# Loads of queries and keys in 1 KB runs, transposed by head, low parts on VectorE, and other weights of a list scheduler: attention and two expert layers on one core

## The chip, the core and the metric

The kernel runs on one core of a Trainium2 chip. The metric is the time of one execution on the device in microseconds (us), and the time before is the median of three runs. Five engines work side by side, each in the order in which its instructions were written: TensorE (PE in the profile, with its weight loads as PEld), VectorE (DVE), ScalarE (ACT), GpSimd (POOL) and SyncE (SP), whose queue issues nearly all DMAs.

## The reference

Three layers follow each other. Attention has 4 batches of 8 heads, 576 positions and 64 values per head, with a causal window of 64 positions. The second layer works on 2304 tokens; the third sends each token whose skip score is positive to one of eight experts.

```python
scores = np.matmul(q, k.transpose(0, 1, 3, 2)) / np.sqrt(D)
scores = np.where((rel >= 0) & (rel < 64), scores, -1e9)
attn = softmax(scores)
x = np.matmul(attn, v)                      # as [2304, 512]
h = x @ w_in                                # [512, 2048], float64 weights
x = (h * np.tanh(np.log1p(np.exp(h)))) @ w_out
e = np.argmax(x @ w_gate, axis=1)           # 8 experts
y = gate * (np.maximum(x @ w1[e], 0) @ w2[e])
out = np.where(x @ w_skip > 0, x + y, x)
```

## The kernel before, in words

The tokens form six blocks of 384 (`NB`), and each block has four pairs of heads. A pair's path is: load queries and keys (`load_nat` for the first eight pairs, `load_dvt` later), transpose them on TensorE into PSUM (`nat_T`, twice, keys and queries), copy them out (`nat_k`, `nat_q`), scores (`att_S`), mask and maximum on VectorE (`att_max`), exponentials on ScalarE (`att_exp`), normalizing (`att_norm`), a transpose (`att_PT`), and the product with the values (`att_PV`). Products that need more than TensorE's short float format take a high and a low part of each operand: `x_part` and `wide_H`/`wide_L` make them, and `expert_H`/`expert_L`, `xs_H`/`xs_L` do so for the third layer. A low part is the operand minus its high part, one subtraction of 128x512 (line 341 or 1082).

The second layer goes over 16 chunks of 128 hidden columns for each block, 96 chunks `c` in all. `L1(c)` is 12 products of 128x384 into a PSUM tile `ph` of two buffers; `m_min`, `m_exp`, `m_square`, `m_ln`, `m_r` and `m_g` form the gate on VectorE and ScalarE, and `m_g` frees `ph`; `L2(c)` adds the result into three PSUM tiles `po`, one for each 128 tokens, over the 16 chunks of the block. In block 0, `L2` takes `g` whole; later it takes high and low parts. At the end of a block `x_evac` copies `po` out to one of only three tiles `xs`, the router finds each token's expert, and `scatter` writes `xs` to a table of slots in memory. So the three `xs` tiles, and with them `po`, wait for the scatters of the block before. A scatter waits until every slot was filled once (`fill_slots`, 17 DMAs in rounds of two, each round behind a write by `fill_zero` and the landing of the round before).

The weights of the second layer come as 64-bit numbers (`wide_load`) and are converted on VectorE and ScalarE (`wide_e`, `wide_a`, `wide_l`, `wide_s`), 32 tiles in the first blocks. After the last block comes the bend to the third layer: router, scatter, and a product with 0/1 matrices (`select`) that gathers the first expert's tokens. Then the experts follow one another.

The order is not written by hand. `Plan` lists tasks with engines and costs, dependencies, buffers and due times; `order` simulates the lists greedily and picks, for the engine that is free first, the ready task with the earliest due time. Due times come from `T0`, `D0`, `D1`, `US`, `UO`, `WO`, `LO` and are shifted by kind of task through `LATE`; the engine of a task is chosen by cost with `PRICE0`, `PRICE`, `PRICE2` (by time) and `LEAN`. `keep_warm` puts small products (`warm`) where the plan has TensorE idle before the first `L2` and in the bend.

The diff touches the tables above, `load_nat`, `nat_T` and task costs:

```python
for r in range(4):
    PE.transpose(o[:, r, :nr], t[:nr, r].rearrange("p j d -> p (j d)"), ident[:nr, :nr])
```

Of the kernel before, what the change touches and what calls it, by code (L numbers as in the profile page):

```python
# [9 lines left out]
F32 = mybir.dt.float32  # L10
# [15 lines left out]
T0, D0, D1, US, UO, WO, LO = 20.57, 3.54, 4.21, 1.68, 5.52, 2.09, 3.4  # L26
# [6 lines left out]
FILL_AT, FILL_BY = 21, 6.0  # L33
# [125 lines left out]
TW0 = 30.94  # L159
PRICE0 = dict(P=0.0, V=2.28, A=0.5, G=-0.5, S=0.0)  # L160
TW = 309.39
PRICE2 = dict(P=0.0, V=1.26, A=2.91, G=0.0, S=0.0)
PRICE = dict(P=0.0, V=2.33, A=1.47, G=0.63, S=0.0)
LAT = {("V", "V"): 0.13, ("A", "A"): 0.13, ("A", "V"): 0.14, ("V", "A"): 0.13, ("P", "P"): 0.05}
LATE = dict(wl=-9.64, wa=-0.1, wo=-3.47, ws=-4.07, wH=-11.22, lqk=-4.23, nT=-11.43, S=-14.23, ex=-0.53, nm=-4.0, PT=0.94, Pe=7.68, xH=-13.18, L1=2.57, L2=0.89, me=1.15, n=-4.49, mn=-0.61, ln=-5.67, r=-7.61, g=3.04, gH=3.02, xe=2.94, rT=1.62, re=-6.31, rl=2.98, rs=-1.25, lg=13.87, ro=-1.68, eH=16.04, rc=1.8, PV=-0.21, wL=2.42, ga=-3.86, sL=-1.97, xo=13.29, eL=4.54, m2=6.01, bl=18.08, wb=-0.93, ke=-20.26, m1=16.67, se2=-11.46, sl=7.64, el=-0.26, qT=2.69, fz=-9.43, bt=-20.62, se=-13.56, sH=11.09, sd=-1.3, wg=-1.88, tg=9.05, fs=-2.81, xgH=-0.09, sm=9.36, oh=-8.74, su=7.71, xL=-4.21, we=3.45, pl=-8.44, gL=2.75, pi=-2.04, co=-1.2, pm=-0.37, dm=8.62, kT=-2.92, fi=-2.37, mx=3.12, L2t=14.66, ep=-14.67, rq=0.13, lv=-0.43)
LEAN = {('kT', 'A'): 0.38, ('qT', 'A'): -1.31, ('nm', 'A'): 0.39, ('xH', 'A'): -1.88, ('wo', 'A'): -0.82, ('wH', 'A'): -0.15, ('n', 'A'): -1.04, ('re', 'A'): -1.33, ('xe', 'A'): 0.36, ('nm', 'G'): 0.37, ('wL', 'G'): -2.59, ('gL', 'G'): 1.14}
SLACK = dict(P=0.04, V=0.0, A=0.0, G=0.17, S=0.0)
# [3 lines left out]
def tile_kernel(  # L171
# [15 lines left out]
    B, H, S, D = q.shape  # L187
# [31 lines left out]
    for p0 in (0, 64):  # L219
        sl = maskA[p0:p0 + 64]  # L220
# [146 lines left out]
    def one(eng, cost):  # L367
        return [(eng[0], eng[1], cost)]
# [44 lines left out]
    def load_nat(pr):  # L413
        blk, hp = divmod(pr, 4)
        nq = rqp.tile([128, 4, 2, D], F32, tag="rk", name="nq", bufs=4)
        nk = rqp.tile([128, 4, 2, D], F32, tag="rk", name="nk", bufs=4)
        r0 = 0
        for g, n, b, s0 in runs(blk):
            t0 = max(s0 - 64, 0)
            nr = (s0 + 192 * n - t0) // 4  # L420
            hs = slice(2 * hp, 2 * hp + 2)
            SP.dma_start(out=nk[r0:r0 + nr], in_=k[b, hs, t0:s0 + 192 * n].rearrange("j (p r) d -> p r j d", r=4))
            SP.dma_start(out=nq[48 * g:48 * (g + n)], in_=q[b, hs, s0:s0 + 192 * n].rearrange("j (p r) d -> p r j d", r=4))
            r0 += nr
        nat[pr] = (nq, nk, r0)

    def nat_T(pr, i):
        t = nat[pr][i]
        nr = nat[pr][2] if i else 96
        if pr < 4:  # L430
            o = ps_o.tile([128, 4, 128], F32, tag=f"po{i}", name="tqk")
        else:
            o = ps_s.tile([128, 4, 128], F32, tag="ps", name="tqk")
        for r in range(4):
            PE.transpose(o[:, r, :nr], t[:nr, r].rearrange("p j d -> p (j d)"), ident[:nr, :nr])
        tqk[pr, i] = o
# [142 lines left out]
    for pr in range(NU // 2):  # L579
        t = unit_time(2 * pr) - 5  # L580
        if pr < NPE:
            T(("lqk", pr), one(SS, 1.8 if len(runs(pr // 4)) == 1 else 2.3), lambda e, pr=pr: load_nat(pr), lat=2.3,
              get=[("rk", ("nq", pr)), ("rk", ("nk", pr))], due=t, t0=.7)
            for i in (1, 0):
                T(("nT", pr, i), one(PP, .36), lambda e, pr=pr, i=i: nat_T(pr, i), after=[("lqk", pr)] + ([("S", pr - 1)] if pr else []),
                  get=[(f"po{i}" if pr < 4 else "ps", ("tqk", pr, i))], use=[("nq", pr) if i == 0 else ("nk", pr)])
        else:
            T(("lqk", pr), one(SS, 3.6 if len(runs(pr // 4)) == 1 else 7.2), lambda e, pr=pr: load_dvt(pr), lat=2.3,
              get=[("rq", ("nq", pr)), ("rk", ("nk", pr))], due=t - 5)
        nd = sum(3 if r[3] == 0 else 2 for r in runs(pr // 4))  # L590
        T(("lv", pr), [("S", SP, max(1.6, .5 * nd))], lambda e, pr=pr: load_v(pr, e), lat=2.3,
          get=[("vt", ("vt", pr))], due=unit_time(2 * pr))
# [104 lines left out]
    for f in range(NF):  # L697
        for kind in ("in", "out"):
# [3 lines left out]
            T(("wl", key), [("S", SP, 1.46)], lambda e, key=key, i=i: wide_load(key, i, e), lat=2.3, due=t - 8)  # L702
# [428 lines left out]
    for n in range(32):  # L1131
# [10 lines left out]
        T(("eL", key), [("G", G, 1.23), ("V", V, .6)], lambda e, key=key: expert_L(e, key), after=[("eH", key)],  # L1142
# [287 lines left out]
```

## Time and profile before

| | |
|---|---|
| median of three runs | 695.97 us (695.02 to 697.1) |
| profiled execution | 695.74 us, of which the span is 693.6 us |
| TensorE busy | 678.2 us, 98% of the span |
| VectorE busy | 450.6 us, 65% |
| ScalarE busy | 392.2 us, 57% |
| GpSimd busy | 74.2 us, 11% |
| mean granted clock of TensorE | 0.991 |

Busy time is what the profiler counts for instructions on each engine; products overlap, so starts tell more than durations. An idle stretch before an instruction is put down to what released it last.

### The profile page before, as it was taken

How to read it: one execution, taken by the hardware profiler on the slowest of the kernel's cores; microseconds unless marked ns; L12 is line 12 of the kernel's file. 1: busy time of each engine (PE TensorE's matmuls, PEld its weight loads, DVE VectorE, ACT ScalarE, POOL GpSimd, SP SyncE). 2: the span in 40 equal slices, each digit the busy share in tenths (PEclk: the TensorE clock that was granted, in tenths of full speed). 3: DMA queues.
4: the chain of work that ended last, by engine and by line, in shares of the span. 5: the costliest groups of instructions: out<-in, count | busy, mean ns of one | idle time of the engine just before them, and what ended most of it. 6: DMA issues, size and time to landing. Idle time of an engine off the chain costs nothing. (4 is left out here: it accounts for less than half of the span.)

```text
span 693.6 us, 13440 instructions
## 1 busy us (share of the span) xinstructions
PE 678.2 (98%) x4884; PEld 582.5 (84%) x4884; DVE 450.6 (65%) x1268; ACT 392.2 (57%) x963; POOL 74.2 (11%) x133
## 2 busy tenths in 40 slices
PE   6899999999999999999999999999999999999996
PEld 6787776788888888888888888888898898998994
DVE  4999999876766556556776656457668563674352
ACT  5899787677667676686555555445552242232130
POOL 3000000000020001000020002013244011020011
PEclk9999999999999999999999999999998999999999
DMA  9999986877432312232311000054473677677200
GB/s 189 270 280 303 267 156 138 202 150 158 79 74 44 83 36 53 46 92 49 78 31 41 30 1 26 1 182 138 129 231 115 228 245 259 238 290 271 89 25 21
DMA packets 150492, 92.53 MB, mean 133 GB/s; under 512 B 111869, under 2 KB 128253, under 8 KB 150416
## 3 DMA queue, kind: packets, MB, share of 16 engines
q1 hardware_dynamic: 147696, 87.11, 47.7%
q0 software_dynamic: 2720, 4.42, 1.8%
q8 instruction: 45, 0.74, 0.5%
q14 instruction: 31, 0.25, 0.1%
HBM read 73.96 MB, written 17.86 MB: 132 GB/s over the span
## 5 line engine op out<-in xcount | busy, mean ns | idle before, releaser
L735 PE MATMUL ph<-xH,w 128*128 128x384 f32 x768 | 220.6, 348 | 0.2
L786 PE MATMUL po<-w,gH 128*128 128x512 f32 x480 | 154.4, 403 | 0.0
L735 PEld LDWEIGHTS ph<-xH,w 128*128 128x128 f32 x768 | 140.9, 188 | 7.0 <-issue 1.9
L735 PE MATMUL ph<-xL,w 128*128 128x384 f32 x384 | 130.0, 338 | 0.0
L743 ACT ACTIVATE u<-u 128x384 f32<-128x384 f32 x96 | 50.3, 524 | 122.2 <-DVE u L740 122.2
L786 PEld LDWEIGHTS po<-w,gH 128*128 128x128 f32 x480 | 87.2, 188 | 17.2 <-issue 1.6
L786 PE MATMUL po<-w,gL 128*128 128x512 f32 x240 | 95.1, 396 | 0.0
L762 DVE SCALAR_TENSOR_TENSOR u<-u,ph 128x384 f32<-128x384 f32 x80 | 44.1, 551 | 71.6 <-ACT u L756 71.2
L735 PEld LDWEIGHTS ph<-xL,w 128*128 128x128 f32 x384 | 72.2, 188 | 4.1 <-issue 2.2
L740 DVE TENSOR_SCALAR u<-ph 128x384 f32<-128x384 f32 x96 | 53.1, 553 | 18.1 <-PE ph L735 17.2
L1218 PEld LDWEIGHTS ph<-xgT,w 128*128 128x128 f32 x512 | 63.8, 190 | 1.0 <-DVE xgT L317 0.4
L1218 PE MATMUL ph<-xgT,w 128*128 128x144 f32 x512 | 64.3, 286 | 0.3 <-DVE xgT L317 0.3
L771 DVE TENSOR_TENSOR gL<-u,gH 128x384 fp32r<-128x384 f32 x80 | 46.5, 581 | 17.2 <-ACT gH L315 14.2
L529 ACT ACTIVATE P<-P,mx 128x128 f32<-128x128 f32 x144 | 55.6, 389 | 0.9 <-DVE mx L522 0.9
L786 PEld LDWEIGHTS po<-w,gL 128*128 128x128 f32 x240 | 45.1, 188 | 11.3 <-DVE gL L771 0.6
L1245 ACT ACTIVATE hH<-ph 128x288 fp32r<-128x288 f32 x32 | 13.2, 411 | 68.9 <-PE ph L1218 56.5
L747 ACT ACTIVATE u<-u 128x384 f32<-128x384 f32 x96 | 50.4, 525 | 2.9
L753 ACT ACTIVATE u<-u 128x384 f32<-128x384 f32 x96 | 50.2, 523 | 2.3
L756 ACT ACTIVATE u<-u 128x384 f32<-128x384 f32 x96 | 50.2, 522 | 2.3
L786 PE MATMUL po<-w,g 128*128 128x512 f32 x96 | 44.0, 594 | 0.0
L1262 PE MATMUL po<-w,hH 128*128 128x512 f32 x128 | 42.6, 414 | 0.0
L341 DVE TENSOR_TENSOR w<-st,w 128x512 fp32r<-128x512 f32 x48 | 34.3, 732 | 0.7
(156 smaller groups left out, 985.6 us busy)
## 6 DMA issues: line engine op xcount, KB each, us to landing
st<-in_moe_w_dram SPq DMA_DIRECT2D x64, 256.0 KB, 6.2
w<-in_moe_w_dram SPq DMA_DIRECT2D x32, 512.0 KB, 5.5
w<-in_moe_w_in_dram SPq DMA_DIRECT2D x16, 512.0 KB, 7.1
w<-in_moe_w_out_dram SPq DMA_DIRECT2D x16, 512.0 KB, 6.6
out_dram<-xs SPq DMA_DIRECT2D x18, 256.0 KB, 2.4
xg<-xg_d SPq DMA_DIRECT2D x16, 257.0 KB, 4.0
ca<-w SPq DMA_DIRECT2D x16, 256.0 KB, 3.7
xg_d<-nothing SPq DMA_DIRECT2D x16, 256.0 KB, 5.0
```

The source lines that it names most:

```text
L529: A.activation(P[:, i], P[:, i], AF.Exp, bias=mx[:, 0, u % 2, i:i + 1], scale=-1.0, accum_out=mx[:, 1, u % 2, i:i + 1])
L735: PE.matmul(phs[c], a[:, kk], b[:, kk], start=kk == 0 and n == 0, stop=kk == NK - 1 and n == len(terms) - 1)
L740: V.tensor_scalar(u, phs[c], 20.0, None, op0=ALU.min)
L743: A.activation(us[c], us[c], AF.Exp)
L747: A.activation(us[c], us[c], AF.Square, bias=1.0)
L753: A.activation(us[c], us[c], AF.Ln, scale=0.5, bias=half_t[c])
L756: A.activation(us[c], us[c], AF.Exp, scale=-1.0)
L762: V.scalar_tensor_tensor(o, us[c], 1.0, phs[c], op0=ALU.subtract, op1=ALU.mult)
L771: eng.tensor_tensor(gL, us[c], gH.bitcast(F32), op=ALU.subtract)
L786: PE.matmul(po[m, t], a[:, ts], b, start=f == 0 and n == 0, stop=f == NF - 1 and n == len(terms) - 1)
L1218: PE.matmul(ph[:, i], w1_t[e, kk][:, 128 * f:128 * f + 128], xgT[e][:, kk, :N1], start=kk == 0, stop=kk == NK - 1)
L1262: PE.matmul(po2[e, s], a[:, f, ss], b, start=f == 0 and n == 0, stop=f == 7 and n == 2)
```

## The change

In the tile of a pair's queries or keys, the four positions of a partition now lie together for each head, so that each run is 256 values long in memory and in the tile; before, the heads alternated, and a run was 64 values. The transposes change with it: for each of the four positions and each of the two heads there is one product with the identity, which writes 64 partitions of the result. The third part moves all low parts of expert weights and of the last block's tokens from a choice of GpSimd or VectorE to VectorE alone. The fourth gives the scheduler other numbers, and fills the slots from time 130 of the plan rather than from the due time of chunk 21.

```diff
-T0, D0, D1, US, UO, WO, LO = 20.57, 3.54, 4.21, 1.68, 5.52, 2.09, 3.4
+T0, D0, D1, US, UO, WO, LO = 0.34, 3.79, 4.58, 0.22, 0.66, 6.96, 1.58
...
-FILL_AT, FILL_BY = 21, 6.0
+FILL_AT, FILL_BY = 130.0, 6.0
...
-PRICE = dict(P=0.0, V=2.33, A=1.47, G=0.63, S=0.0)
+PRICE = dict(P=0.0, V=2.92, A=1.11, G=0.63, S=0.0)
...
-        nq = rqp.tile([128, 4, 2, D], F32, tag="rk", name="nq", bufs=4)
+        nq = rqp.tile([128, 2, 4 * D], F32, tag="rk", name="nq", bufs=4)
...
-            SP.dma_start(out=nk[r0:r0 + nr], in_=k[b, hs, t0:s0 + 192 * n].rearrange("j (p r) d -> p r j d", r=4))
+            SP.dma_start(out=nk[r0:r0 + nr], in_=k[b, hs, t0:s0 + 192 * n].rearrange("j (p r) d -> p j (r d)", r=4))
...
         for r in range(4):
-            PE.transpose(o[:, r, :nr], t[:nr, r].rearrange("p j d -> p (j d)"), ident[:nr, :nr])
+            for j in range(2):
+                PE.matmul(o[64 * j:64 * j + 64, r, :nr], t[:nr, j, D * r:D * r + D], ident[:nr, :nr], start=True, stop=True)
...
-            T(("lqk", pr), one(SS, 1.8 if len(runs(pr // 4)) == 1 else 2.3), lambda e, pr=pr: load_nat(pr), lat=2.3,
+            T(("lqk", pr), one(SS, 1.3 if len(runs(pr // 4)) == 1 else 2.0), lambda e, pr=pr: load_nat(pr), lat=2.3,
...
-                T(("nT", pr, i), one(PP, .36), lambda e, pr=pr, i=i: nat_T(pr, i), after=[("lqk", pr)] + ([("S", pr - 1)] if pr else []),
+                T(("nT", pr, i), one(PP, .44), lambda e, pr=pr, i=i: nat_T(pr, i), after=[("lqk", pr)] + ([("S", pr - 1)] if pr else []),
...
-        tf = chunk_time(FILL_AT) + FILL_BY * (n // 2)
+        tf = FILL_AT + FILL_BY * (n // 2)
...
-        T(("sL", t), [("G", G, 1.23), ("V", V, .6)], lambda e, t=t: xs_L(e, t), after=[("sH", t)], use=[("xs", L, t)],
+        T(("sL", t), one(VV, .6), lambda e, t=t: xs_L(e, t), after=[("sH", t)], use=[("xs", L, t)],
...
-        T(("eL", key), [("G", G, 1.23), ("V", V, .6)], lambda e, key=key: expert_L(e, key), after=[("eH", key)],
+        T(("eL", key), one(VV, .6), lambda e, key=key: expert_L(e, key), after=[("eH", key)],
```

The tables `TW0`, `PRICE0`, `TW`, `PRICE2`, `LATE`, `LEAN` and `SLACK` have other numbers too, and three costs of DMA issues (`lv`, `wl`, `fs`) are raised. Lines from 434 on stand one line lower in the change. Three places show how the order moves.

The first is the start of SP's queue. `nk` and `nq` are keys and queries, `vt` values, `w` a weight tile as it comes from memory. Before:

```order
L641 DMA w_159<-in_moe_w_in_dram 128x4x256
L422 DMA nk<-in_k_dram 96x8x64
L423 DMA nq<-in_q_dram 96x8x64
L422 DMA nk<-in_k_dram 96x8x64
L423 DMA nq<-in_q_dram 96x8x64
L404 DMA vt<-in_v_dram 64x2x64
L411 DMA vt<-in_v_dram 128x5x64 x2
L422 DMA nk<-in_k_dram 96x8x64
L423 DMA nq<-in_q_dram 96x8x64
L641 DMA w_288<-in_moe_w_in_dram 128x4x256
```

And now:

```order
L642 DMA w_159<-in_moe_w_in_dram 128x4x256
L422 DMA nk<-in_k_dram 96x2x256
L423 DMA nq<-in_q_dram 96x2x256
L642 DMA w_165<-in_moe_w_in_dram 128x4x256
L422 DMA nk<-in_k_dram 96x2x256
L423 DMA nq<-in_q_dram 96x2x256
L645 DMA w_243<-in_moe_w_out_dram 128x1024
L422 DMA nk<-in_k_dram 96x2x256
L423 DMA nq<-in_q_dram 96x2x256
L642 DMA w_311<-in_moe_w_in_dram 128x4x256
L404 DMA vt<-in_v_dram 64x2x64
```

The second weight tile moved ahead of the second pair, a tile of `w_out` ahead of the third pair, and the first values moved behind them.

The second place is the last fill of the slots on SP's queue (`xg_d<-nothing`, the 128x16x2 form is the last of the 17). Before:

```order
L476 DMA rq<-in_q_dram 32x12x32
L479 DMA rk<-in_k_dram 32x12x32
L978 DMA xg_d<-nothing 128x4x128 x2
L981 DMA xg_d<-nothing 128x16x2
L404 DMA vt<-in_v_dram 64x2x64
L411 DMA vt<-in_v_dram 128x5x64 x2
```

And now:

```order
L477 DMA rq<-in_q_dram 32x6x32
L480 DMA rk<-in_k_dram 32x6x32
L979 DMA xg_d<-nothing 128x4x128 x2
L404 DMA vt<-in_v_dram 64x2x64
L411 DMA vt<-in_v_dram 128x5x64 x2
L982 DMA xg_d<-nothing 128x16x2
L477 DMA rq<-in_q_dram 32x6x32
```

The last fill moved behind the loads of one more pair's values, which themselves wait for a buffer until an earlier pair's product with the values is done. On VectorE the write ahead of this fill stood after 29 of the 96 gate products (`m_g`) and now stands after 34. On ScalarE the copies out of block 1's `po` stood behind the gate work of 34 chunks and one of the three now stands behind that of 37. TensorE's `L2(32)`, the first product into the same `po` for block 2, stood behind `L1(34)` and now stands behind `L1(38)`.

The third place is VectorE at the bend (`xs<-po` copies the last block out, `xsL` and `w<-st,w` are low parts). Before:

```order
L830 TENSOR_SCALAR xs<-po 128x512
L317 CAST xsH<-xs 128x512
L830 TENSOR_SCALAR xs<-po 128x512
L317 CAST xsH<-xs 128x512
L317 CAST w_6546<-st 128x512
L341 TENSOR_TENSOR w_6546<-st,w_6546 128x512
L830 TENSOR_SCALAR xs<-po 128x512
L317 CAST xsH<-xs 128x512
L896 TENSOR_REDUCE r_mx<-lp 128x1
```

And now:

```order
L831 TENSOR_SCALAR xs<-po 128x512
L317 CAST xsH<-xs 128x512
L1083 TENSOR_TENSOR xsL<-xs,xsH 128x512
L317 CAST xsH<-xs 128x512
L1083 TENSOR_TENSOR xsL<-xs,xsH 128x512
L317 CAST w_6630<-st 128x512
L831 TENSOR_SCALAR xs<-po 128x512
L341 TENSOR_TENSOR w_6630<-st,w_6630 128x512
L897 TENSOR_REDUCE r_mx<-lp 128x1
L317 CAST xsH<-xs 128x512
```

The low parts of the tokens came to VectorE, one of the three copies went to ScalarE, and the subtraction for an expert weight moved behind the last copy.

## Rows read from the trace of the kernel before

**Rows 1.** Busy time by stretch: PE, PEld, DVE, ACT, POOL, then TensorE's granted clock.
```profile
5.18:45.18 40.00, 33.76 (x504) 29.70 (x503) 33.50 (x123) 31.96 (x101) 3.08 (x22) 0.96 1.14 247
...
425.00:527.00 102.00, 102.00 (x573) 89.64 (x572) 63.83 (x147) 52.07 (x102) 28.11 (x27) 1.00 0.41 132
527.00:540.00 13.00, 11.67 (x88) 11.12 (x87) 10.20 (x55) 2.25 (x6) 7.61 (x8) 0.74 0.17 65
```

**Rows 2.** Instructions in order of time (start, duration): the first gate, and a wait ahead.
```profile
16.57 0.43 DVE L650 TENSOR_SCALAR cv<-w 128x512 int32<-128x512 int32 x1 [2.48 <-DMA w<-in_moe_w_in_dram]
...
45.18 0.55 DVE L762 SCALAR_TENSOR_TENSOR g<-u,ph 128x384 f32<-128x384 f32 x1
```

**Rows 3.** Stretches of 1 us at the start; the last two columns are DMA share and GB/s.
```profile
16.00:17.00 1.00, 0.00 (x0) 0.00 (x0) 0.43 (x2) 0.24 (x1) 0.00 (x0) 1.00 1.15 160
...
24.00:25.00 1.00, 1.00 (x18) 0.99 (x17) 1.00 (x3) 1.00 (x5) 0.00 (x0) 1.00 1.22 294
```

**Rows 4.** Groups of VectorE instructions by form, 5.1 to 45.7 us: busy us, mean ns.
```profile
L656 DVE SCALAR_TENSOR_TENSOR ca<-w,cv 128x512 int32<-128x512 int32 x8 | 5.4, 682 | 0.1
...
L545 DVE TENSOR_TENSOR P<-P,mx 128x384 f32<-128x384 f32 x8 | 4.2, 552 | 0.0
L650 DVE TENSOR_SCALAR cv<-w 128x512 int32<-128x512 int32 x8 | 3.6, 450 | 6.6 <-DMA w<-in_moe_w_in_dram 6.6
L673 DVE CUSTOM_DVE_ANT_0 ca<-ca,cv 128x1024 uint16<-128x1024 uint16 x5 | 3.4, 684 | 0.7 <-ACT cv L663 0.7
...
L317 DVE CAST w<-ca 128x512 fp32r<-128x512 f32 x3 | 1.3, 421 | 0.0
...
L317 DVE COPY qT<-tqk 128x384 f32<-128x384 f32 x1 | 0.8, 841 | 0.0
```

**Rows 5.** TensorE in order of time: transposes, products of half width, products of full width.
```profile
9.80 0.55 PE L435 MATMUL tqk<-ident,nk 96*128 96x96 f32 x4
10.18 0.49 PE L435 MATMUL tqk<-ident,nq 96*128 96x96 f32 x4
...
36.87 0.92 PE L561 MATMUL pv<-PT,vt 128*64 128x64 f32 x24
37.72 0.44 PE L735 MATMUL ph<-xH,w 128*128 128x384 f32 x1
...
520.62 1.05 PE L1071 MATMUL sel<-ident,base 128*128 128x128 f32 x8
521.42 0.72 PE L786 MATMUL po<-w,gH 128*128 128x512 f32 x2
```

**Rows 6.** In order of time, around the bend.
```profile
527.50 1.64 DVE L341 TENSOR_TENSOR w<-st,w 128x512 fp32r<-128x512 f32 x1
527.74 0.96 PE L871 MATMUL lp<-wgs,xf 128*128 128x9 f32 x8
...
529.07 0.68 DVE L830 TENSOR_SCALAR xs<-po 128x512 f32<-128x512 f32 x1
...
529.80 0.66 PE L841 MATMUL rtp<-ident,xs 128*128 128x128 f32 x4 [1.04 <-DVE xs L830]
...
530.29 3.11 PE L871 MATMUL lp<-wgs,xf 128*128 128x9 f32 x16
```

**Rows 7.** The page's groups: subtractions for low parts on VectorE.
```profile
L341 DVE TENSOR_TENSOR w<-st,w 128x512 fp32r<-128x512 f32 x48 | 34.3, 732 | 0.7
```

**Rows 8.** DMA issues (count, KB, us to landing): the last fill, the scatters of block 0.
```profile
xg_d<-nothing SPq DMA_DIRECT2D x1, 16.0 KB, 4.3
...
xg_d<-xs,r_si POOLq DMA_INDIRECT x3, 4.1
```

**Rows 9.** In order of time, the end of block 1: TensorE, ScalarE.
```profile
216.27 0.33 PE L735 MATMUL ph<-xH,w 128*128 128x384 f32 x1
...
216.56 1.06 ACT L828 ACTIVATE xs<-po 128x512 f32<-128x512 f32 x2
...
218.39 0.62 PE L786 MATMUL po<-w,gH 128*128 128x512 f32 x2
```

More of the change, by code (lines that the diff above doesn't have):

```diff
@@ L156, in emit @@
             self.tasks[k]["fn"](e[1])
[L159 to L162, printed above, removed]
-PRICE = dict(P=0.0, V=2.33, A=1.47, G=0.63, S=0.0)
+TW0 = 24.45
+PRICE0 = dict(P=0.0, V=2.35, A=0.23, G=-0.5, S=0.0)
+TW = 308.65
+PRICE2 = dict(P=0.0, V=2.12, A=3.83, G=0.0, S=0.0)
+PRICE = dict(P=0.0, V=2.92, A=1.11, G=0.63, S=0.0)
 LAT = {("V", "V"): 0.13, ("A", "A"): 0.13, ("A", "V"): 0.14, ("V", "A"): 0.13, ("P", "P"): 0.05}
-LATE = dict(wl=-9.64, wa=-0.1, wo=-3.47, ws=-4.07, wH=-11.22, lqk=-4.23, nT=-11.43, S=-14.23, ex=-0.53, nm=-4.0, PT=0.94, Pe=7.68, xH=-13.18, L1=2.57, L2=0.89, me=1.15, n=-4.49, mn=-0.61, ln=-5.67, r=-7.61, g=3.04, gH=3.02, xe=2.94, rT=1.62, re=-6.31, rl=2.98, rs=-1.25, lg=13.87, ro=-1.68, eH=16.04, rc=1.8, PV=-0.21, wL=2.42, ga=-3.86, sL=-1.97, xo=13.29, eL=4.54, m2=6.01, bl=18.08, wb=-0.93, ke=-20.26, m1=16.67, se2=-11.46, sl=7.64, el=-0.26, qT=2.69, fz=-9.43, bt=-20.62, se=-13.56, sH=11.09, sd=-1.3, wg=-1.88, tg=9.05, fs=-2.81, xgH=-0.09, sm=9.36, oh=-8.74, su=7.71, xL=-4.21, we=3.45, pl=-8.44, gL=2.75, pi=-2.04, co=-1.2, pm=-0.37, dm=8.62, kT=-2.92, fi=-2.37, mx=3.12, L2t=14.66, ep=-14.67, rq=0.13, lv=-0.43)
@@ L170, in tile_kernel @@
+LEAN = {('kT', 'A'): 1.28, ('qT', 'A'): -0.66, ('nm', 'A'): 0.76, ('xH', 'A'): -1.89, ('wo', 'A'): -0.74, ('wH', 'A'): -0.98, ('n', 'A'): -1.4, ('re', 'A'): -2.12, ('xe', 'A'): -0.06, ('nm', 'G'): 1.83, ('wL', 'G'): -2.63, ('gL', 'G'): -0.13}
+SLACK = dict(P=0.13, V=0.0, A=0.0, G=0.17, S=0.0)
 @with_exitstack
@@ L414, in load_nat @@
         blk, hp = divmod(pr, 4)
-        nq = rqp.tile([128, 4, 2, D], F32, tag="rk", name="nq", bufs=4)
-        nk = rqp.tile([128, 4, 2, D], F32, tag="rk", name="nk", bufs=4)
+        nq = rqp.tile([128, 2, 4 * D], F32, tag="rk", name="nq", bufs=4)
+        nk = rqp.tile([128, 2, 4 * D], F32, tag="rk", name="nk", bufs=4)
         r0 = 0
@@ L421, in load_nat @@
             hs = slice(2 * hp, 2 * hp + 2)
-            SP.dma_start(out=nk[r0:r0 + nr], in_=k[b, hs, t0:s0 + 192 * n].rearrange("j (p r) d -> p r j d", r=4))
-            SP.dma_start(out=nq[48 * g:48 * (g + n)], in_=q[b, hs, s0:s0 + 192 * n].rearrange("j (p r) d -> p r j d", r=4))
+            SP.dma_start(out=nk[r0:r0 + nr], in_=k[b, hs, t0:s0 + 192 * n].rearrange("j (p r) d -> p j (r d)", r=4))
+            SP.dma_start(out=nq[48 * g:48 * (g + n)], in_=q[b, hs, s0:s0 + 192 * n].rearrange("j (p r) d -> p j (r d)", r=4))
             r0 += nr
@@ L701, in tile_kernel @@
             t = chunk_time(f if kind == "in" else f + 2) - WO
-            T(("wl", key), [("S", SP, 1.46)], lambda e, key=key, i=i: wide_load(key, i, e), lat=2.3, due=t - 8)
+            T(("wl", key), [("S", SP, 1.62)], lambda e, key=key, i=i: wide_load(key, i, e), lat=2.3, due=t - 8)
             T(("we", key), one(VV, .34), lambda e, key=key: wide_e(key), after=[("wl", key)],
@@ L983, in tile_kernel @@
     for n in range(NS + 1):
-        tf = chunk_time(FILL_AT) + FILL_BY * (n // 2)
+        tf = FILL_AT + FILL_BY * (n // 2)
         if n % 2 == 0:
             T(("fz", n), one(VV, .2), lambda e: fill_zero(), due=tf, t0=tf, after=[("fs", x) for x in range(max(n - 2, 0), n)])
-        T(("fs", n), one(SS, 1.9 if n < NS else 1.0), lambda e, n=n: fill_slots(n), after=[("fz", n - n % 2)], lat=5, due=tf + 2)
+        T(("fs", n), one(SS, 2.0 if n < NS else 1.0), lambda e, n=n: fill_slots(n), after=[("fz", n - n % 2)], lat=5, due=tf + 2)
     T(("wg",), one(SS, 1.0), lambda e: load_wgs(), due=chunk_time(2), lat=3)
```

5 lines of the change are left out of this document (2 added, 3 removed).

## The prediction

> **What bounds the kernel now.** The first view is the table of stretches [rows 1]. From 425 to 527 us TensorE is busy the whole time, 102.00 of 102.00 us, at a granted clock of 1.00, while VectorE works 63.83 us. So an engine beside TensorE has some 38 us to spare there, and what it gains or loses is worth nothing until TensorE has to wait for it. In the first 40 us the opposite holds: VectorE works 33.50 of 40.00 us and TensorE's 33.76 us are partly `warm` products, which lead nowhere. What ends that stretch is read from the instructions in order [rows 2]: the first `m_g` starts on VectorE at 45.18 us, and the first `L2` and all that follows stand behind it. The third view, the order around the bend, shows the only other place where TensorE stands still for long: the stretch 527 to 540 has a mean granted clock of 0.74 [rows 1], TensorE waits 1.04 us there for the copy `xs` of VectorE at line 830, and the 16 rows of `lp` that follow take 3.11 us where 8 rows took 0.96 a little earlier [rows 6]. Hence four terms: the first gate (A), products added to a TensorE that has no free time (B), the bend (C), and waits that could open at the end of block 1 (D). Everything else that moves lies beside a busy TensorE.
>
> **A, the first gate.** VectorE has more to do before it now, by the order of the two kernels: one weight tile and a half more to convert, which is two `wide_e` of 0.450, two `wide_a` of 0.682 and two more sums and subtractions of 0.684 (these shapes stand in [rows 4]); one more normalizing product of 0.552; two key copies come to it and one query copy leaves, of 0.841 each; three casts of 0.421 go to ScalarE. That is 0.90 + 1.36 + 1.37 + 0.55 + 0.84 - 1.26 = 3.75 us more. Against it stands what VectorE idles, 40.00 - 33.50 = 6.50 us [rows 1], and nearly all of that is 6.6 us ahead of line 650, put down to the arrival of weight tiles [rows 4]; one wait of 2.48 us ends at 16.57 [rows 2]. The second weight tile was the tenth DMA of SP's queue and is now the fourth. It passes one pair's two loads and the values ahead of it: a pair's loads of 96x512 numbers of 4 bytes are 393 KB together, 2.5 us at the 160 GB/s that the 256-byte runs reach at 16 us [rows 3]. So the wait of 2.48 us goes. Of the other 4.1 us I take 1.6 us away, because the pairs between the weights come in 1 KB runs too, and where tiles of weights come in such runs the traffic is 294 GB/s [rows 3]. With that VectorE loses 4.05 us of idle time and gains 3.75 us of work: **-0.3 us**. The ends: with no idle time lost, +3.75; with 5.5 of the 6.5 us lost (about 1 us of first arrivals must stay), -1.75. Neither the 1 KB runs by themselves nor the ten groups of transposes ahead of this gate are paid: VectorE's chain, not TensorE, sets its time, and a group of four transposes is 0.38 us, 9.80 to 10.18 [rows 5].
>
> **B, more products on TensorE.** A group of four transposes becomes eight products with the identity, two for each position, each on 64 of the 128 columns. Six of the eight pairs are transposed before or around the first gate; the four groups of the last two pairs fall where TensorE has no free time. A product of this kind leaves two rows: `att_PV` has 12, and stands as 24 in 0.85 us (36.87 to 37.72 [rows 5]), 35 ns for a row of 64 values, in halves that run beside each other. `select`'s product with the identity, of full width, takes 0.80 us for 8 rows of 128 values (520.62 to 521.42 [rows 5]), 100 ns each. For these pairs a row has 96 or 112 values, 104 in the mean: 81 ns by the second, halved 41 if the halves run beside each other. I take 42 ns, nearest to the half-width row since the halves are laid out as there: 16 rows are 0.67 us, 0.29 more than 0.38, four times 1.2; a swap of one pair's transposes with another's products makes it **+1.3 us**. The ends: 35 ns a row, four times (0.56 - 0.38) = +0.7; 100 ns a row, four times (1.60 - 0.38) = 4.9, so +5.0.
> The trace has half-width and full-width products next to each other (37.72 follows 36.87 at the usual pace [rows 5]), but no row prices the change between them apart. The Trainium skill (TensorEngine Tiling (Array Packing), Key Properties) says that a change of the tiling mode drains TensorE, which speaks against this edit: each group goes into half-width mode and out again. If each of the eight changes cost one row of 0.10 us, an estimate of mine for that rule, B would be 2.1 instead of 1.3 us; no run here shows it.
>
> **C, the bend.** Two things go. VectorE ran an expert's subtraction of 1.64 us at 527.50, where the mean of that form is 0.732 [rows 6, 7], and the last copy `xs` stood behind it until 529.07. In the new order the copy stands ahead of that subtraction, and GpSimd, which had low parts of its own at the time (7.61 of 13 us busy [rows 1]), has none: the copy comes about 0.9 us earlier. If with that TensorE's wait of 1.04 us goes, the 16 rows of `lp` may keep the full clock: 8 rows were 0.96, so 16 are 1.9 at most, and 1.2 to 1.5 us of their 3.11 are saved. I take -0.9 and -1.5. One thing comes: subtractions for `xsL` on VectorE, one of them between the copies and the router's maximum, 0.7 us. Sum **-1.7 us**. The ends: all of the wait, the clock and the faster copy together, 1.04 + 1.5 + 0.9 = -3.4; nothing gained and one more subtraction of 0.73 with 0.3 of cast ahead of the router, +1.0.
> The other half of this edit, 16 expert subtractions from GpSimd to VectorE, is 16 x 0.732 = 11.7 us [rows 7] in a stretch where VectorE has 38 us free and TensorE none [rows 1]: nothing. If that cover failed, TensorE would be seen waiting for `w` ahead of expert products; in the trace of before it never does between 425 and 527.
>
> **D, the last fill.** Block 0's scatters wait for the last fill, block 1's copies `xs` wait for these scatters, and `L2(32)` waits for the copies. The fill's write now stands after 34 gate products, so it runs at about the end of `L2(31)`; ahead of the fill on SP is also a load of values that waits for a buffer until a product with values is done. I put its issue 3 us after `L2(31)` (one `L1` and one such product: 2.12, 216.27 to 218.39 [rows 9], and 0.85). Then 4.3 until it lands, 4.1 for a scatter [rows 8] and 1.06 for a copy [rows 9]: 12.5 us. On TensorE there are now five `L1` between `L2(31)` and `L2(32)`, where there was one: 5 x 2.12 = 10.6, and two products with values, 1.7, so 12.3 us, to which scores and transposes come. That nearly meets: I take **+0.5 us**. The ends: 0; and with another scatter behind the first, not beside it, 4.1 + 0.5 and some, +5.0.
>
> Fewer GpSimd operations, casts that go from VectorE to ScalarE, 30 more `warm` products and the other order of some loads: nothing, as long as TensorE's rows stay dense from the first gate to the bend.
>
> **Sum.** -0.3 + 1.3 - 1.7 + 0.5 = -0.2 us against the profiled execution of 695.74 us (span 693.6): **695.5 us**. The median of the runs, 695.97, lies 0.2 above that execution. About 0.3%, 2.1 us, is what can be told from no change here; so my forecast is no measurable change.
>
> **The rivals.**
> Faster: A and C both come near their good ends, -1.4 and -3.3, with B and D as above less a little: 692.2 us. For it speaks that nearly all of VectorE's idle time is one kind of wait [rows 4], and the half clock of `lp` [rows 6]; against it, 3.75 us of added work that is certain, and that a wait of 1 us in the bend may only change its name.
> Slower, by D: the third `xs` tile comes free later than the five `L1` and what stands between them last (some 15 us after `L2(31)` with scores and transposes). Then TensorE stands still for what is over, up to 4 or 5 us, with its clock to fall on top: 699 us. For it speaks the chain of 12.5 us just worked out; against it, that scatters of one block can land beside each other, and more attention between.
> Slower, by B: the halves do not run beside each other, so each row costs 81 to 100 ns. It decides from about 96 ns on, where B alone adds 3.4 us over what I took: 699 us. `att_PV` speaks against it.
> Slower, by A: the weight tiles land no earlier, VectorE idles as before, and the 3.75 us stand: 699.5 us. This is also the case in which the change does not do what it says: the runs are 1 KB, yet the weights moved ahead of the pairs take the time that the runs save, and the pairs land when they did; if VectorE finds other work meanwhile, that ends at no change.
>
> **How the numbers follow.** No measurable change 0.42, the sum with all its terms inside their middles (the even exchange in A counts here). Faster 0.33, since two terms, A and C, can each bring 1 to 2 us more than I took. Slower 0.25: D 0.12, B 0.08, A 0.05. The forecast is the likeliest case, 695.5. The range goes to 692.0 below, the good ends of A and C together, and to 699.5 above, any one of the three slower cases whole; two of them together, or both good ends with B at its lowest, are the 2 in 10 left out.
>
> **What would show it.** A is right if the first `m_g` starts at 44 to 46 us and the idle time ahead of line 651 is 2 to 3 us instead of 6.6; an idle time still over 6 means the loads do not land earlier. B is right if a group of transposes after the gate takes 0.6 to 0.75 us from start to next start; 1.3 or more means that the halves run one after the other. C is right if TensorE has no wait over 0.5 us for line 831 and the 16 rows of `lp` take under 2 us; if they take 3 us again at half clock, only the copy's time was gained. D is right if TensorE's rows between `L2(31)` and `L2(32)` have no gap over 1 us; a gap there that ends with a copy `xs` is the rival. The whole is wrong if TensorE, between the first gate and 527 us, shows gaps that sum to over 3 us anywhere else, or if the span after the bend changes by more than 1 us.

## The result, and the profile after

The changed kernel took 703.27 us (median of 4 runs, 702.9 to 704.67), the kernel before 696.54 us beside it (695.02 to 697.8). The ratio is 1.0101, with a 95% interval of 1.008 to 1.0121: **slower by 0.8 to 1.2%**, where no measurable change was forecast, and above the end of the range.

The span of the profiled execution is 701.5 us, 7.9 more than before. TensorE's rows cut it into four pieces, here from the starts of rows. The "third chunk" is the first product of the third `L1`, which waits for the first gate; the stretch from there to the last product of the last `L2` is where TensorE has no free time; the bend goes on to the first product of the experts.

| | before | after | longer by |
|---|---|---|---|
| third chunk starts | 45.78 | 48.84 | 3.06 |
| stretch to the last `L2` product | 481.28 (to 527.06) | 488.49 (to 537.33) | 7.21 |
| bend | 12.93 (to 539.99) | 10.07 (to 547.40) | -2.86 |
| rest of the span | 153.6 | 154.1 | 0.5 |

So the start and the stretch both cost more than forecast, and the bend gave more. The start first: VectorE in order of time, changed kernel, waits and the first gate.

```profile
5.00 0.43 DVE L651 TENSOR_SCALAR cv<-w 128x512 int32<-128x512 int32 x1 [3.91 <-DMA w<-in_moe_w_in_dram]
...
9.94 0.55 DVE L651 TENSOR_SCALAR cv<-w 128x512 int32<-128x512 int32 x1 [2.35 <-DMA w<-in_moe_w_in_dram]
...
47.77 0.54 DVE L763 SCALAR_TENSOR_TENSOR g<-u,ph 128x384 f32<-128x384 f32 x1
```

The first gate starts at 47.77, 2.59 us later than in [rows 2]. The wait for the second weight tile has not gone: it comes at 9.94 instead of 16.57 and lasts 2.35 instead of 2.48 us. Busy time of the engines (PE, PEld, DVE, ACT, POOL, then the granted clock) from 5.18 us, where [rows 1] begins, to the gate, to be held against the first of [rows 1]:

```profile
5.18:47.77 42.59, 37.42 (x636) 33.27 (x636) 36.50 (x128) 33.76 (x104) 3.03 (x22) 1.00 1.01 256
```

VectorE works 36.50 us where it worked 33.50, and idles 6.09 where it idled 6.50. The transposes, in TensorE's order, before and after:

```profile
48.01 0.55 PE L435 MATMUL tqk<-ident,nk 112*128 112x112 f32 x4
48.39 0.49 PE L435 MATMUL tqk<-ident,nq 96*128 96x96 f32 x4
48.72 0.62 PE L786 MATMUL po<-w,g 128*128 128x512 f32 x1
```
```profile
47.26 0.99 PE L436 MATMUL tqk<-ident,nk 112*64 112x112 f32 x16
48.07 0.83 PE L436 MATMUL tqk<-ident,nq 96*64 96x96 f32 x16
48.84 0.44 PE L736 MATMUL ph<-xH,w 128*128 128x384 f32 x1
```

A pair takes 1.58 us where it took 0.71. In the stretch TensorE has one long wait, which the kernel before did not have. TensorE, ScalarE, GpSimd and SP's queue of the changed kernel there:

```profile
236.29 0.44 PE L736 MATMUL ph<-xH,w 128*128 128x384 f32 x1 [2.33 <-DVE u L763]
```
```profile
234.69 0.49 ACT L315 ACTIVATE xH<-pv 128x384 fp32r<-128x384 f32 x1 [2.92 <-remote]
235.08 0.51 ACT L757 ACTIVATE u<-u 128x384 f32<-128x384 f32 x1
...
236.65 0.58 ACT L829 ACTIVATE xs<-po 128x512 f32<-128x512 f32 x1
```
```profile
230.27 1.17 POOL L277 DMA_INDIRECT xg_d<-xs,r_si  x1 [6.97 <-DMA rq<-in_q_dram]
...
234.17 0.51 POOL L833 COPY xs<-tok 128x1 int32<-128x1 int32 x2 [0.19 <-issue]
```
```profile
224.87 0.47 SPq L982 DMA_DIRECT2D xg_d<-nothing  x1
```

The last fill goes out at 224.87 (188.95 before). The first scatter follows 5.4 us later, at 230.27, against 196.26 before. The tags `xs<-tok`, which need the free `xs` tiles, end at 234.17 + 0.51 = 234.68, and at 234.69 ScalarE goes on after 2.92 us without work. Behind it are the last step of a gate (line 757), the gate product on VectorE, and the `L1` at 236.29. TensorE stood still for 2.33 us. What held ScalarE, the changed kernel's trace calls "remote". A kernel with the same late fill (the run below with the start's numbers as before) names it: there ScalarE waits for the landing of a scatter, ahead of a copy `xs`.

```profile
230.63 0.60 ACT L829 ACTIVATE xs<-po 128x512 f32<-128x512 f32 x1 [2.76 <-DMA xg_d<-xs,r_si]
```

The bend went as forecast or better (TensorE, to be held against [rows 6]):

```profile
538.00 0.96 PE L872 MATMUL lp<-wgs,xf 128*128 128x9 f32 x8
...
538.87 0.61 PE L842 MATMUL rtp<-ident,xs 128*128 128x128 f32 x4
539.31 1.91 PE L872 MATMUL lp<-wgs,xf 128*128 128x9 f32 x16
...
547.40 0.76 PE L1219 MATMUL ph<-xgT,w 128*128 128x144 f32 x4 [0.29 <-issue]
```

There is no wait for a copy `xs`, and the 16 rows of `lp` take 1.91 us instead of 3.11.

Of the stretch's 7.21 us the rows so far explain 2.50 in waits (2.33 and one of 0.17), 2 x 0.87 = 1.74 for the two pairs transposed in it, and 0.14 for one product with values (0.85) that now lies in it while one old pair of groups (0.71) lies ahead. **2.83 us are left**. Some of that is still waiting: an idle time counts from a modelled end, and from start to start the wait at 236.29 costs 2.50 us (2.67 since the row before, where 0.18 is usual), the one of 0.17 costs 0.32, and a shorter one at 226.09 costs 0.24. That makes 3.06 instead of 2.50, and leaves some 2.3 us with TensorE busy. The experiments had to find them.

### The profile page after: what moved, and what is told of

It reads as the page before. It is cut to its first block, busy times and chain, and to the rows that moved or that the text cites. A ratio compares the mean times of both kernels' runs of the same rounds, so it can differ in the third digit from the quotient of the medians.

```text
span 701.5 us, 13871 instructions
## 1 busy us (share of the span) xinstructions
PE 685.4 (98%) x5106; PEld 585.0 (83%) x5106; DVE 452.1 (64%) x1268; ACT 401.1 (57%) x980; POOL 49.2 (7%) x114
## 5 line engine op out<-in xcount | busy, mean ns | idle before, releaser
L736 PE MATMUL ph<-xH,w 128*128 128x384 f32 x768 | 222.9, 351 | 2.4 <-DVE u L763 2.3
L772 DVE TENSOR_TENSOR gL<-u,gH 128x384 fp32r<-128x384 f32 x80 | 44.4, 555 | 11.4 <-ACT gH L315 9.2
L341 DVE TENSOR_TENSOR w<-st,w 128x512 fp32r<-128x512 f32 x64 | 43.2, 687 | 1.6 <-ACT w L315 0.6
```

Of the source, the lines that this page charges most:

```text
L341: eng.tensor_tensor(l, raw_w.pop(key), h.bitcast(F32), op=ALU.subtract)
L736: PE.matmul(phs[c], a[:, kk], b[:, kk], start=kk == 0 and n == 0, stop=kk == NK - 1 and n == len(terms) - 1)
L772: eng.tensor_tensor(gL, us[c], gH.bitcast(F32), op=ALU.subtract)
```

## The experiments

The suspicion came from counting: scores, products with values and `lq` (products for the router) write 64 columns of the array or fewer, half its width, and so do the new transposes. TensorE goes into such a group and out again, one visit, 33 times in the stretch before, and 47 times after, since scores and products with values, which stood side by side in 18 places, now mostly stand apart:

```profile
221.70 0.33 PE L736 MATMUL ph<-xH,w 128*128 128x384 f32 x1
221.97 0.92 PE L562 MATMUL pv<-PT,vt 128*64 128x64 f32 x24
222.81 0.89 PE L507 MATMUL sc<-kT,qT 64*64 64x128 f32 x24
223.63 0.44 PE L736 MATMUL ph<-xH,w 128*128 128x384 f32 x1
223.91 0.34 PE L736 MATMUL ph<-xL,w 128*128 128x384 f32 x1
224.09 0.51 PE L736 MATMUL ph<-xH,w 128*128 128x384 f32 x2
```

Here (changed kernel, one of the few places with both) starts of `L1` rows are 0.18 us apart (223.91 to 224.09), but 0.27 on the way in (221.70 to 221.97) and 0.28 after the way out (223.63 to 223.91).

**The halves alone.** The kernel before with the new tiles, loads and transposes; the order on every engine is that of before.

```diff
-            PE.transpose(o[:, r, :nr], t[:nr, r].rearrange("p j d -> p (j d)"), ident[:nr, :nr])
+            for j in range(2):
+                PE.matmul(o[64 * j:64 * j + 64, r, :nr], t[:nr, j, D * r:D * r + D], ident[:nr, :nr], start=True, stop=True)
```

> The kernel before with one part of the change alone: queries and keys in 1 KB runs and eight half-width products for each group of transposes; the order on every engine stays that of before. Theory (TensorE has no free time after the first gate, so dearer transposes are paid in full): three pairs are transposed behind the first gate, and in the trace of the change a pair's two groups take 1.58 us from start to next start (47.26 to 48.84) where they took 0.71 before (48.01 to 48.72), so 3 x 0.87 = 2.6 us more, 698 to 699 us against 696; the last product of the second layer starts 2 to 3 us later than at 526.6. Rival (loads in 1 KB runs land earlier and pull the first gate forward by as much or more): the first gate before 44 us, and 694 to 696.5 us in all.

Measured: 697.05 us beside 696.80, ratio 1.0001 (0.9986 to 1.0016). Third chunk and last `L2` product:

```profile
43.96 0.45 PE L736 MATMUL ph<-xH,w 128*128 128x384 f32 x1
...
528.00 0.40 PE L787 MATMUL po<-w,gL 128*128 128x512 f32 x1
```

The stretch is 484.04 us, 2.76 longer: three pairs at 0.92. The theory holds there. But the whole is no longer than before, between what the theory gave and what the rival gave, and the bend (12.99) is that of before. So by the medians the start gave back about as much, as the rival said; in this profile the third chunk is 1.8 us earlier. That the 1 KB runs did this is not shown: kernels with the old loads and the old order of the start began the third chunk anywhere between 44.08 and 47.46.

**Low parts on VectorE alone**, in the kernel before.

```diff
-        T(("eL", key), [("G", G, 1.23), ("V", V, .6)], lambda e, key=key: expert_L(e, key), after=[("eH", key)],
+        T(("eL", key), one(VV, .6), lambda e, key=key: expert_L(e, key), after=[("eH", key)],
```

The three tasks for the tokens (`sL`) are changed in the same way.

> The kernel before with one part of the change alone: all low parts on VectorE. Theory (the change's gain at the bend, 9.8 us from the last product of the second layer to the first of the experts where it was 12.7, comes from this part): the copy ahead of the router no longer waits for a subtraction of 1.6 us, the 16 rows of lp run at the full clock in about 1.9 us, and the whole is 2 to 3 us shorter, about 693.5 us. Rival (the gain comes from the other numbers of the scheduler, which moved a copy to ScalarE and the subtraction behind it): 695 to 697 us, lp at half clock as before. Second rival (the 16 subtractions added to VectorE are paid): 699 us and more.

Measured: **692.57 us beside 696.80**, ratio 0.9945 (0.9926 to 0.9963). TensorE at the bend:

```profile
528.57 0.40 PE L786 MATMUL po<-w,gL 128*128 128x512 f32 x1
...
530.63 1.91 PE L871 MATMUL lp<-wgs,xf 128*128 128x9 f32 x16
...
538.17 1.11 PE L1218 MATMUL ph<-xgT,w 128*128 128x144 f32 x6 [0.30 <-DVE xgT L317]
```

The bend is 9.60 us against 12.93. The gain at the bend belongs to this part, and this part alone makes a kernel that is faster than both. The medians differ by 4.2 us, more than the 3.3 at the bend and the 2 to 3 of the theory; where the rest lies is not shown.

**Sixty products of half width, and sixty of full width.** The kernel before with one small product ahead of each `L1` of chunks 24 to 83; the control has 128 columns.

```diff
+            if 24 <= c < 84 and kk == 0:
+                PE.matmul(ph_all[:64, TB:], ones8[:, :64], ones8, start=True, stop=True)
```

> The kernel before, and ahead of the first product of each of the chunks 24 to 83 one small product more, of 64 columns out of 128 (half width), that leads nowhere: 60 more visits to the half-width mode, where the change has 14 more than the kernel before (47 against 33). Theory (each change between full and half width costs time of its own, about 0.09 us on the way in, 0.12 on the way out and 0.10 on the first product after): some 0.3 us each beside the row's own 0.06, so 60 x 0.36 = 22 us, about 718 us; if some fall beside visits that are there anyway, 715. Rival (the width costs nothing and the change's time went elsewhere): 60 x 0.06 = 3.6 us, the same as the run with full-width products, 700 us.

> The control for the run with 60 half-width products: the same 60 small products in the same places, of 128 columns, so with no change of width. Theory and rival alike: 60 rows of about 0.06 us and a little for the other number format, 700 to 702 us. The difference between the two runs, over 60, is the price of one visit to half width: 0.25 to 0.3 us by the theory, 0 by the rival.

Measured: 716.99 and 702.04 us, ratios 1.0301 (1.0271 to 1.0331) and 1.0084 (1.0057 to 1.0111), the first between the theory's 715 and 718. The difference is 14.95 us, **0.25 us for each of the sixty** beyond the product itself. Three of them stand beside an `lq`, so there are 57 visits more, 0.26 us each. In the rows, half width first, then full:

```profile
311.06 0.40 PE L789 MATMUL po<-w,gL 128*128 128x512 f32 x1
311.38 0.24 PE L736 MATMUL ph<-ones 128*64 128x128 bf16 x1
311.56 0.44 PE L738 MATMUL ph<-xH,w 128*128 128x384 f32 x1
```
```profile
303.76 0.40 PE L789 MATMUL po<-w,gL 128*128 128x512 f32 x1
304.00 0.23 PE L736 MATMUL ph<-ones 128*128 128x128 bf16 x1
304.04 0.42 PE L738 MATMUL ph<-xH,w 128*128 128x384 f32 x1
```

From the `L2` product to the `L1` product it is 0.50 us with half width and 0.28 with full. The Trainium skill (TensorEngine Tiling (Array Packing), Key Properties) says that a change of tiling mode drains TensorE. This pair of runs agrees, with 0.25 to 0.26 us for the way in and out together.

**Scores and products with values apart**, in the kernel before: one due time as changed.

```diff
-LATE = dict(..., S=-14.23, ...)
+LATE = dict(..., S=5.18, ...)
```

> The kernel before with one due time as changed (S, the scores: 5.18 instead of -14.23): scores and the product with the values stand apart in all pairs, and TensorE visits half width 53 times behind the third L1 chunk instead of 33; fills, layout and low parts as before. Theory (by the rows, two visits apart cost 0.19 us more than one visit of both; 0.25 by the runs with 60 products): the stretch from the third L1 chunk to the last L2 grows by 3.8 to 5 us over 481.3, the whole 699.5 to 701.5 us against 696. Rival (the run with the attention's due times put back gained only 0.8 us net of its waits, so visits cost little in this kernel): less than 1.5 us more, 696 to 697.5 us.

Measured: 699.83 us beside 696.19, ratio 1.0062 (1.0041 to 1.0083).

```profile
47.46 0.44 PE L735 MATMUL ph<-xH,w 128*128 128x384 f32 x1
...
532.25 0.40 PE L786 MATMUL po<-w,gL 128*128 128x512 f32 x1
```

The stretch is 484.79 us, 3.51 longer for 20 visits more, 0.18 each: a little under the range given, and far from the rival. At that price the 14 visits more in the changed kernel are 2.5 us. Two of the 14 are the transposes' own, though, whose way out already stands in the 1.74, so 2.1 is nearer. With the 0.56 that the waits cost beyond their idle times, that is about the 2.83 us left over.

**The change with one part undone.** Old loads and transposes; fills from time 98; the attention's due times (S, PT, Pe, PV) as before; the numbers for the start as before.

```diff
-FILL_AT, FILL_BY = 130.0, 6.0
+FILL_AT, FILL_BY = 98.0, 6.0
```

(This one is the second; the first is the first experiment's diff backwards on the changed kernel, the third and fourth set only table entries back.)

> The changed kernel with one part undone: loads and transposes of queries and keys as before (256-byte runs, four full-width transposes a group), the order of the change on every engine. Theory (the halves are paid only behind the first gate): two pairs lie behind the third L1 chunk here, 2 x 0.87 = 1.7 us less, and one pair just ahead of it, up to 0.9 us less: the stretch from the third L1 chunk to the last L2, 488.5 us in the change, becomes 486 to 487, and the whole 701 to 702 us against 703.3. Rival (the 1 KB runs were holding the start up, or pulling it forward): the first gate moves by more than 1.5 us from 47.8, and the whole by 3 us or more either way.

> The changed kernel with the fills of the slots from time 98 of the plan rather than 130, so that the last fill's write stands after 27 gate products instead of 34. Theory (TensorE's 2.3 us of waiting at 234 us comes from GpSimd's scatters behind that fill): the gap goes, the stretch from the third L1 chunk to the last L2 is 2.0 to 2.7 us shorter than 488.5, the whole 700.5 to 701.5 us. Rival (the wait is ScalarE's, for some other buffer): the gap stays, 703 us.

> The changed kernel with the due times of four attention tasks as before (scores S, transposed probabilities PT and their copy Pe, product with the values PV): scores and product with the values stand side by side again, and TensorE visits half width 38 times behind the first gate instead of 47; the fills stay late. Theory (0.25 us a visit, from the runs with 60 products): the stretch from the third L1 chunk to the last L2 is 9 x 0.25 = 2.2 us shorter than 488.5, 486 to 486.7, and the whole about 701 us unless the start moves. Rival (the visits are not where the change's time went): the stretch stays within 0.7 us of 488.5.

> The changed kernel with the scheduler's numbers for the start as before (T0, D0, D1, US, UO, WO, LO, TW0 and PRICE0); all else as changed, and 38 visits to half width, as it falls out. Theory (the later first gate is VectorE's, which has more key copies and conversions ahead of it because of these numbers): the first gate at 43.5 to 45.5 us instead of 47.8, 2.3 to 4 us; with 9 visits fewer 2.2 us more; the fills still late, so part of the 2.3 us gap stays: the whole 697 to 699.5 us. Rival (the halves or the 1 KB runs make the gate late): the gate stays at 47 us or later, the whole 701 us.

| undone | third chunk | stretch | bend | median beside 696.11 | ratio (interval) |
|---|---|---|---|---|---|
| nothing (the change) | 48.84 | 488.49 | 10.07 | 703.27 beside 696.54 | 1.0101 (1.008 to 1.0121) |
| transposes | 48.20 | 486.19 | 11.23 | 700.76 | 1.0065 (1.0045 to 1.0086) |
| late fill | 47.06 | 484.90 | 10.06 | 698.18 | 1.0041 (1.0021 to 1.006) |
| attention's due times | 48.88 | 486.53 | 10.07 | 702.38 | 1.0095 (1.0067 to 1.0123) |
| start's numbers | 47.52 | 489.81 | 10.08 | 703.04 | 1.01 (1.0072 to 1.0127) |

The old transposes take 2.30 us out of the stretch, within what the theory gave; 0.9 of it is waits, which sum to 2.50 us in the changed kernel's stretch and to 1.64 here. The early fill takes out 3.59, more than the 2.0 to 2.7 expected: no wait of TensorE is left in the stretch, and GpSimd's first scatter starts at 195.95. The whole is even 5.1 us shorter than that of the changed kernel. But 1.78 of this is the start, and the start cannot be the fill's doing, since up to the first gate every engine has the same instructions in the same order in both kernels. The attention's due times take out 1.96 with nine visits fewer, as the theory said, but 1.4 of these are waits, which are shorter in that order; of the visits themselves this run shows only 0.6 and is no clean measure, and the whole, 702.38, is above the 701 expected. With the start's numbers as before the first gate is at 45.13, inside the theory's range, but two kernels that keep the changed start have it at 45.99 (the early fill) and 46.09 (the last run below), so this shows 0.9 to 2.6 us for these numbers. The whole gained nothing, where the theory gave 697 to 699.5. Two rows show why, the third chunk behind a pair's transposes, and the fill's wait, now longer:

```profile
45.13 0.55 DVE L763 SCALAR_TENSOR_TENSOR g<-u,ph 128x384 f32<-128x384 f32 x1
```
```profile
46.74 0.85 PE L436 MATMUL tqk<-ident,nq 96*64 96x96 f32 x15
47.52 0.44 PE L736 MATMUL ph<-xH,w 128*128 128x384 f32 x1
...
231.29 0.45 PE L736 MATMUL ph<-xH,w 128*128 128x384 f32 x1 [4.08 <-DVE u L763]
```

Behind this wait the granted clock is 0.50 from 231.82 to 235.23, which the wait of 2.33 us in the changed kernel did not bring.

**Three parts undone at once.**

> The changed kernel with three parts undone at once: old loads and transposes, fills from time 98, due times of four attention tasks as before; the scheduler's numbers for the start and the low parts on VectorE stay. 36 visits to half width. Theory (these three make all of the longer stretch): from the third L1 chunk to the last L2 481.5 to 483 us as in the kernel before, the bend 10 to 11, and the whole at 695 to 698 us, what is left over being the start. Rival (something else lengthens the stretch): 484.5 us or more, 700 us.

Measured: 698.61 us beside 696.19, ratio 1.0038 (1.002 to 1.0057).

```profile
51.55 0.44 PE L735 MATMUL ph<-xH,w 128*128 128x384 f32 x1
...
532.46 0.39 PE L786 MATMUL po<-w,gL 128*128 128x512 f32 x1
```

The stretch is 480.91 us, what it was before (481.28). These three make the longer stretch. One at a time they took out 2.30 + 3.59 + 1.96 = 7.85, together 7.58, but that these agree so well is partly luck: each of the three also shortened the one long wait, which can go only once. The stretch is 0.6 us below the range given and the whole 0.6 us above it, because the start is later still, at 51.55, and that eats more than the bend's 2.87. This start is neither kernel's own: VectorE works 39.2 us from its first conversion to the gate here, 36.7 in the changed kernel and 33.5 before, and idles 6.9 us. Which numbers of the scheduler cost what there is not shown.

**Low parts shared with GpSimd again**, in the changed kernel: the second experiment's diff backwards.

> The changed kernel with its low parts shared between GpSimd and VectorE again (19 of them go to GpSimd); in this order no subtraction for an expert weight stands ahead of the last copy out of the bend. Theory of the prediction (two causes at the bend: the copy behind the subtraction, and a GpSimd that slows VectorE's operations): the copy is free but VectorE's operations are slower than with an idle GpSimd, the bend 11 to 12.5 us against 10.1, the whole 704.5 to 706 us. Rival (only the place of the subtraction counted): the bend at 10 to 10.5 us, the whole 703 to 704 us.

Measured: 707.58 us beside 696.19, ratio 1.019 (1.0134 to 1.0245). The bend is 13.31 us and the whole is longer too than the theory gave, though no expert subtraction stands ahead of the last copy there. VectorE, GpSimd and TensorE at that bend:

```profile
540.82 1.68 DVE L341 TENSOR_TENSOR w<-st,w 128x512 fp32r<-128x512 f32 x1
...
542.68 0.96 DVE L914 SCALAR_TENSOR_TENSOR first<-r_z,r_d 128x8 f32<-128x8 f32 x1
```
```profile
540.49 1.46 POOL L341 TENSOR_TENSOR w<-st,w 128x512 fp32r<-128x512 f32 x1
541.91 1.71 POOL L1083 TENSOR_TENSOR xsL<-xs,xsH 128x512 fp32r<-128x512 f32 x1
```
```profile
540.52 1.91 PE L872 MATMUL lp<-wgs,xf 128*128 128x9 f32 x16
...
544.10 0.17 PE L930 MATMUL pp<-r_oh,triu 128*128 128x8 bf16 x1 [1.23 <-DVE r_oh L922]
```

A subtraction takes 1.68 us on VectorE beside GpSimd's, and an operation of 8 columns 0.96; this one ends at 543.64, and GpSimd's subtraction beside it at 543.62. TensorE then waits 1.23 us. What the clock does there is in the next rows, the bend of this kernel and of the changed one (the column ahead of the last two is the granted clock):

```profile
538.60:551.90 13.30, 11.51 (x93) 10.95 (x91) 10.38 (x56) 1.82 (x5) 7.77 (x7) 0.74 0.17 64
```
```profile
537.30:547.40 10.10, 9.45 (x101) 8.81 (x99) 8.81 (x57) 2.23 (x6) 2.97 (x3) 1.00 0.22 83
```

The mean clock is 0.74 with GpSimd's low parts and 1.00 without, as it was 0.74 in the kernel before [rows 1]. The last copy was free to go early here, and yet the bend was long: what the bends of some 13 us share is GpSimd at work. The 16 rows of `lp`, though, take 1.91 us here too, so their gain comes from the copy's place and not from GpSimd. The Trainium skill (SBUF — State Buffer, Who interferes with whom) says that a VectorE instruction with two inputs in SBUF contends with a GpSimd instruction that reads SBUF. The rows agree, and line 341 has a mean of 687 ns in the changed kernel and 686 in the kernel before with low parts on VectorE alone, where it was 732 [rows 7].

The clock is a cause of its own. With the old transposes the bend was 11.23 us (table above) though GpSimd has no low parts there and TensorE's rows in the bend come in the same order:

```profile
534.39:545.62 11.23, 10.76 (x101) 10.26 (x100) 8.79 (x57) 2.23 (x6) 2.99 (x3) 0.85 0.20 76
```

The granted clock is 0.50, the lower of its two levels, from 538.61 to 542.02, while TensorE, as in the changed kernel, had no wait listed since the last `L2` product. Why it fell in one kernel and not in the other is open.

The stretch of the last run is longer as well, 491.42 us, and its start 1.69 earlier. TensorE waits 2.03 us at 524.42, for a cause not followed here, and 1.12 us at 502.55 for the router, where VectorE is slow beside a GpSimd subtraction that lasts from 500.40 to 501.68:

```profile
500.60 1.12 DVE L906 TENSOR_TENSOR r_z<-lg,r_mx 128x24 f32<-128x24 f32 x1
```

So GpSimd's low parts can also cost time ahead of the bend.

## Why the prediction was wrong

**A, forecast -0.3, measured 2.6 to 3.1 in these two profiles, and about 1.5 over more kernels.** The 3.75 us of added work were nearly right (3.00). The failed step is "VectorE loses 4.05 us of idle time": it lost 0.41. Of the 6.6 us in [rows 4] one wait had ended at 5.18, where the stretch of [rows 1] begins, so only 2.48 lay inside; I counted both as idle time that could go. And this wait did not go: the tile comes 6.6 us earlier, and VectorE asks for it as much earlier. How much of A is the change's own, two profiles do not settle. Five kernels have the old loads and, up to the gate, VectorE's order of before (before, low parts alone, both runs with sixty products, scores apart); three have the changed order on every engine (the change, the early fill, low parts on GpSimd). From the first conversion to the gate VectorE works 33.2 to 33.6 us in the five and 36.5 to 36.7 in the three, but idles 4.9 to 8.0 and 4.1 to 6.1, in the mean 6.5 and 4.9. So the work came nearly as forecast, of the idle time some 1.6 went and not 4.05, and the gate is 1.5 us later in the mean. The upper bound, +3.75, held, and these two profiles lie near it.

**B, forecast 1.3, measured 1.9 in the change.** The 42 ns a row was too little: 0.81 and 0.77 us for 16 rows are 48 to 51 ns. The range held. In the order of before, with three pairs in the stretch, the same edit cost 2.76. That it could be given back at the start I had excluded; the medians of the run with the halves alone say that it was given back in the order of before, while in the order of the change the old transposes made the whole 2.5 us shorter.

**The missing term, some 2.2 us of visits.** The failed step is "Everything else that moves lies beside a busy TensorE": the new order of TensorE's own instructions is on no term, and it made the busy stretch longer. The prediction had read that a change of width costs time, and set it against the transposes alone, at 0.10 a change. It never counted who else changes width: separating scores from products with values brings some 12 more visits, at 0.18 us and up. The order of TensorE's instructions told the number without any run. The prediction also says that no row prices the change; the trace of the kernel before has such rows, with 0.26 us on the way into a group of scores where `L1` rows start 0.18 apart:

```profile
70.16 0.33 PE L735 MATMUL ph<-xH,w 128*128 128x384 f32 x1
70.42 0.89 PE L506 MATMUL sc<-kT,qT 64*64 64x128 f32 x24
```

**C, forecast -1.7, measured -2.86.** The mechanism was named rightly: no wait for `xs`, and `lp` at the full clock. But the size of GpSimd's part was underrated, since it held more than the subtraction (an operation of 8 columns for 0.96 us), and -3.4 was the nearer end. That the clock stayed at 1.00 through the whole bend was not certain, as the 11.23 us with the old transposes show. The cost of nothing for 16 subtractions on VectorE held: the second experiment's stretch (482.42), less its waits of 1.23 at 65.9 and 83.5 us, is no longer than before.

**D, forecast 0.5, measured 2.5.** The failed step is "I put its issue 3 us after `L2(31)`": that chunk's last product starts at 218.86, the fill goes out at 224.87, 6 us later, and the first scatter follows 5.4 us after, not 4.3. Where the trace has the landing of this fill (three of the runs with the late fill), the scatter begins 0.96 to 1.00 us behind it, a step that the sum did not have. The place was wrong too: in the changed kernel it was not `L2(32)` that waited for the copies, but ScalarE, in whose queue the gate of a chunk stood beside them, and so `L1`. I had not asked what is queued behind the waiting copies. That ScalarE waits for a scatter is shown in the run with the start's numbers; for the changed kernel itself it is inferred, with the early fill, where the wait is gone. With the old transposes, and with the attention's due times as before, `L2(32)` does wait for the copies as forecast, 0.51 and 1.10 us.

With the measured pieces the sum is 3.06 + 7.21 - 2.86 + 0.5 = 7.9 us; the medians differ by 6.7, so these two profiles overstate the change by about 1 us, most likely at the start. Two of the slower rivals, A and D, came true in part; I had set them up as alternatives, but they added up, with each other and with B.

## What to carry to other kernels

Where TensorE has no free time, count how often its order goes from full to half width and back, and let products of half width stand together: here one visit cost 0.18 to 0.26 us, as much as a product of 384 columns or more. When a wait is moved earlier, ask whether its demand moves with it; only a wait that lies inside the stretch that is summed may be taken off. And when a change has many parts, try the ones apart: here one, low parts off GpSimd, made the kernel 0.55% faster alone, and was buried under others that cost 1.5%.

## What the runs showed that was not expected

- Going to half width and back costs 0.25 us beyond the products (60 against 60), or 0.26 if only the 57 new visits count, and 0.18 us where one visit is split into two.
- GpSimd's subtraction beside VectorE's stretches it from some 0.69 to 1.68 us, and even one of 8 columns to 0.96.
- The start moves by itself: with VectorE's order unchanged ahead of it, the first gate began at 45.18, 45.54, 44.39, 43.47 and 46.85 us in five kernels with the old loads, and at 47.77, 45.99 and 46.09 in three with the changed start, so one profile cannot settle two microseconds there. What moves it is open.
- The clock of the bend can fall without GpSimd: 0.85 in the mean with the old transposes, 1.00 in the changed kernel, with the same rows of TensorE.
